# An attention and low-rank mixer kernel whose steps are written out as one list in place of loops

## The chip, the cores and the metric

The kernel runs on one core of one Trainium2 chip. The time is the device time of one execution in microseconds (us). A core has five instruction streams that run side by side and meet at semaphores: TensorE (PE in the profile, with its weight loads shown apart as PEld), VectorE (DVE), ScalarE (ACT), GpSimd (POOL) and SyncE (SP). Transfers are issued from SP, ACT or POOL and carried by 16 shared DMA engines. Each stream works through its own instructions in order; an instruction that waits holds up whatever stands behind it.

## The reference

There are 8 batches, 8 heads, 576 tokens, 64 elements per head, and 16 extra "beacon" keys and values ahead of the tokens. Attention is causal over the tokens; the beacons are seen by all. Then a low-rank mix over tokens (rank 32) and a two-layer network over the 512 channels, with 2048 hidden ones.

```python
k_all = concatenate([beacon_k, k], axis=2)
v_all = concatenate([beacon_v, v], axis=2)
scores = where(causal, -1e9, q @ k_all.T / sqrt(64))
a = exp(scores - scores.max(-1)); a /= a.sum(-1) + 1e-9
x = (a @ v_all) arranged as [batch, token, 8 * 64]
u = x + (x.T @ U @ V).T
out = u + maximum(u @ w_ch1, 0) @ w_ch2
```

## The kernel before, in words

Work on the attention goes by pairs of heads: 4 pairs per batch, 32 pairs, numbered 0 to 31. For a pair,

- k and q are loaded, rounded to 16 bits and regrouped (`regroup`, L230) into a tile of three rotating ones, so that a transpose gives both heads at once;
- PE transposes them into PSUM (L238, L240), and DVE copies the result into `kT` and `qT` (L241, L242). From batch 3 on the transposes are done by DMA from SP instead (`turn_heads` L253, `turn_pair` L260), and DVE reorders the result (L268);
- scores are made in two visits of PE (L294): the first for groups 0 and 1, the second for 2 and 3. ACT takes their exponentials into `expt` (L300), and DVE cuts off the masked part (L281, L283);
- for each head PE multiplies with v (L318), v having a column of ones for the sum, and DVE takes the reciprocal and normalises into `xb` (L326, L327).

When the four pairs of a batch are done, `mix_units` makes the low-rank part: a head (L358, with a cast of its small result, L364), then two parts (L377, L384) whose results ACT and DVE copy into `uT` (L391 to L395). `uT` is a ring of token columns. Each 512 of them make a block of the two-layer network, nine blocks in all: 16 units of the first product (`g_unit`, 4 matmuls each, L418, ReLU shared by ACT and DVE), then 16 units of the second (`c_unit`, L434, each output tile of 128 tokens in four units). These units wait in `queue`, and `fill(n)` emits up to n of them between attention steps, so that PE has work while ACT and DVE treat the scores. An empty queue makes `fill` do nothing.

All PSUM tiles come from one ring of eight. The exponentials of a pair use two of four buffers.

The order is that of the emitted program, engine by engine. Before the change it comes from loops: the first two pairs are written out, then a loop over the pairs of batches 0 and 1 (in which pair p+2 is transposed and scored while pair p is multiplied, with the fill counts in `FIRST`), then a loop over the other pairs with nine fill places each. `mix` puts the three mixing steps of a batch into the queue with the gaps of `GAPS`.

Loads of batch 0: k and q come raw in 32 bits by SP and one ACT issue, in four sets of two heads (`load_first`), and are cast by `group_first` on ACT, DVE or POOL. v of batch 0, and everything of the later batches, comes by POOL's queue, which converts to 16 bits. The order there is: v of batch 0 first half, (POOL casts), v second half, k and q of batch 1 in halves, the beacon keys, v of batch 1 first half, the first weight in two pieces, (casts of U and V on POOL), v of batch 1 second half, the second weight in two pieces, batch 2. U and V themselves come by eight small loads from SP (`small_loads`). `keep_warm` emits matmuls whose result is not used: ten ahead of the first transposes and two or three ahead of the first visits (23 in all).

Of the kernel before, what the change touches and what calls it, by code (L numbers as in the profile page):

```python
# [27 lines left out]
def kernel(  # L28
# [103 lines left out]
    def small_loads():  # L132

        f = utp.tile([P, (NT + 1) * R + S], F32, name="small", tag="ut")
        uf, vf = f[:, 0 : (NT + 1) * R].rearrange("p (j r) -> p j r", r=R), f[:, (NT + 1) * R :]
        nc.vector.memset(uf[0:Nb, 0, :], 0.0)
        nc.sync.dma_start(out=uf[Nb:P, 0, :], in_=moe_U[0 : nq[0], :])
        nc.sync.dma_start(out=uf[: nq[0], NT, :], in_=moe_U[0 : nq[0], :])
        nc.sync.dma_start(
            out=uf[:, 1 : NT - 1, :], in_=moe_U[q0[1] : QM, :].rearrange("(j p) r -> p j r", p=P)  # L140
        )
        nc.sync.dma_start(out=uf[:NL, NT - 1, :], in_=moe_U[QM:S, :])
        for cc in range(NCC):
            nc.sync.dma_start(out=vf[ds(R * cc, R), :], in_=moe_V)
# [87 lines left out]
    def qkT_units(L, pr, qT, kT, c):  # L232
# [3 lines left out]
        def one(i, dst, w):  # L236
# [4 lines left out]
            nc.vector.tensor_copy(out=dst[:, c, 0 : w - 4 * P], in_=ps[:, 0 : w - 4 * P])  # L241
            nc.vector.tensor_copy(  # L242
# [22 lines left out]
    def order_units(raw, qT, kT, c):  # L265

        def one(i, dst, w):
            nc.vector.tensor_copy(  # L268
# [130 lines left out]
    def mlp_units(t0, n, dst, flip, turned=True, last=False):  # L399
# [28 lines left out]
        def c_unit(i, part):  # L428
            m = min(P, n - P * i)
            if part == 0:  # L430
                cps["t"] = pst([P, DM], F32, name="cps")
            ps = cps["t"]
            for dc in range(4 * part, 4 * part + 4):
                nc.tensor.matmul(  # L434
                    ps[:m, :], gT["t"][:, dc, ds(P * i, m)], w2[:, dc, :], start=(dc == 0),
                    stop=turned and dc == NDC - 1, skip_group_check=True,
                )
            if part == 3:
                ob = outp.tile([P, DM], F32, name="ob", tag="ob")
                if not turned:  # L440
                    for cc in range(NCC):
                        nc.tensor.matmul(
                            ps[:m, ts(cc, P)], uT[:, cc, ds(ring(t0) + P * i, m)], ident, start=False, stop=True,
                            skip_group_check=True,
                        )
                if turned:
                    nc.vector.tensor_tensor(out=ob[:m, :], in0=ps[:m, :], in1=gT["u"][:m, i, :], op=ALU.add)  # L447
# [4 lines left out]
                nc.sync.dma_start(out=dst(i, m), in_=ob[:m, :])  # L452

        def half_unit(i, h, part):
            cs = ds(DM // 2 * h, DM // 2)
            if part == 0:
                cps["t"] = pst([P, DM // 2], F32, name="cps")
            ps = cps["t"]
            for dc in range(8 * part, 8 * part + 8):
                nc.tensor.matmul(  # L460
                    ps, gT["t"][:, dc, ds(P * i, P)], w2[:, dc, cs], start=(dc == 0), stop=(dc == NDC - 1)
                )
            if part == 1:
                ob = outp.tile([P, DM // 2], F32, name="ob", tag="ob")
                nc.vector.tensor_tensor(out=ob, in0=ps, in1=gT["u"][:, i, cs], op=ALU.add)
                nc.sync.dma_start(out=dst(i, P)[:, cs], in_=ob)

        units += [lambda dc=dc: g_unit(dc) for dc in range(NDC)]
        for i in range((n + P - 1) // P):
            if last and i == 3:  # L470
                units += [lambda h=h, part=part: half_unit(3, h, part) for h in range(2) for part in range(2)]
                continue
            units += [lambda i=i, part=part: c_unit(i, part) for part in range(4)]
# [30 lines left out]
    def load_batch(b):  # L504
        Ls[b] = qk_tiles()
        emit_loads(b, Ls[b], vss[b % 2])

    HALVES = [slice(0, H // 2), slice(H // 2, H)]
    SETS = [slice(2 * c, 2 * c + 2) for c in range(NH2)]
    raw = {}  # L510
# [26 lines left out]
    def act_copy(out, in_):  # L537
        nc.scalar.activation(out=out, in_=in_, func=AF.Copy)

    prs = {}  # L540

    def group_first(c, i, copy):

        if c not in prs:
            prs[c] = pair_tile()
        regroup(Ls[0], c, i, copy, prs[c])
        hs = SETS[c]
        copy(out=Ls[0][0][i][:NL, hs, :], in_=raw["head"][:NL, i, hs, :])

    def regroup_of(p):  # L550
        b, c = divmod(p, NH2)
        prs[p] = pair_tile()
        for i in range(2):
            regroup(Ls[b], c, i, nc.vector.tensor_copy, prs[p])

# [5 lines left out]
    def new_qT(b):  # L561
        qTs[b] = qkt.tile([P, NH2, S], F16, name="qT", tag="qT")

    def new_qT_of(p):
        b, c = divmod(p, NH2)
        if b not in qTs:
            new_qT(b)

    raw_of = {}

    def turn_of(p):
        b, c = divmod(p, NH2)
        new_qT_of(p)
        if c == 0:
            turn_heads(Ls[b], qTs[b], kTs[b % 2])
        regroup_of(p)
        raw_of[p] = turn_pair(prs[p])

    def qkT_of(p):
        b, c = divmod(p, NH2)  # L580
        new_qT_of(p)
        if p in raw_of:
            return order_units(raw_of[p], qTs[b], kTs[b % 2], c)
        return qkT_units(Ls[b], prs[p], qTs[b], kTs[b % 2], c)

    def scores_of(p):
        b, c = divmod(p, NH2)
        return score_units(c, qTs[b], kTs[b % 2], [expts[(2 * p + i) % NE] for i in range(2)])

    def av_of(p):  # L590
        b, c = divmod(p, NH2)
        if c == 0:
# [3 lines left out]
        return [  # L596
            lambda i=i: av_unit(b, 2 * c + i, expts[(2 * p + i) % NE], vss[b % 2], xbs[b]) for i in range(2)
        ]


    NF = 2
    HB = 3
    HX = 3
    AHEAD = 8
    GAPS = [(0, 3, 3), (0, 3, 3), (5, 7, 2)]
    HINT = 5

    FIRST = [0, 0, 0, 0, 10, 5, 4, 4]

    QUOTA = {2: 4}  # L610

    IDLE = [10, 3, 2, 2]
# [3 lines left out]
    def fill(n):  # L616
        while n > 0 and queue:
            u = queue.pop(0)
            if u is not None:
                u()  # L620
            n -= 1

    def feed(b):

        while state["t"] < NBLK and 512 * (state["t"] + 1) <= S * (b + 1):
            t = state["t"]
            queue.extend(
                mlp_units(512 * t, 512, lambda i, m, t=t: rows[ds(512 * t + P * i, m), :], t % 2, t > 0, t == NBLK - 1)
# [3 lines left out]
    def mix(b):  # L632

        head, parts = mix_units(xbs[b], S * b, xts.get(b))
        seq, rest = [], queue[:]
        for u, n in zip([head] + parts, GAPS[min(b, NF)]):
            seq += rest[:n] + [u]
            rest = rest[n:]
        queue[:] = seq + rest
        feed(b)  # L640

    with tc.manual_schedule(engines={ENG.PE, ENG.Activation, ENG.DVE, ENG.SP, ENG.Pool}):
        load_first()
        v_loads(v[0], beacon_v[0], vss[0], HALVES[0])
        cast_small = small_loads()
# [5 lines left out]
        V, G = nc.vector.tensor_copy, nc.gpsimd.tensor_copy  # L651
        group_first(0, 0, act_copy)
        group_first(0, 1, V)
        keep_warm(pst([P, 512], F32, name="idle"), IDLE[0])
        t0, sc = qkT_of(0), scores_of(0)
        for u in t0:
            u()
        sc[0](IDLE[1])
        sc[1]()
        masks = sc[2]  # L660
        group_first(1, 0, G)
        group_first(1, 1, V)
        v_loads(v[0], beacon_v[0], vss[0], HALVES[1])
        for u in qkT_of(1):
            u()
        sc = scores_of(1)
        sc[0](IDLE[2])
        group_first(2, 0, G)

        Ls[1] = qk_tiles()  # L670
        group_first(3, 0, G)
        k_loads(1, Ls[1], HALVES[0])
        q_loads(1, Ls[1], HALVES[0])
        beacon_load(nc.gpsimd, beacon_k[1], Ls[1][0][0], ALLH)
        k_loads(1, Ls[1], HALVES[1])
        q_loads(1, Ls[1], HALVES[1])
        v_loads(v[1], beacon_v[1], vss[1], HALVES[0])
        emit_w1(0)
        emit_w1(1)
        cast_small()  # L680
        v_loads(v[1], beacon_v[1], vss[1], HALVES[1])
        emit_w2()

        NP1 = NF * NH2
        for p in range(NP1):
            b, c = divmod(p, NH2)
            if c == 0 and NF <= b + 1:
                load_batch(b + 1)
            seq = [masks]
            if p + 1 < NP1:  # L690
                seq.insert(0, sc[1])
                masks = sc[2]
            av, qk, sc = av_of(p), [], []
            if p + 2 < NP1:
                if p == 0:
                    seq.append(lambda: group_first(2, 1, V))
                elif p > 1:
                    seq.append(lambda p=p: regroup_of(p + 2))
                qk = [lambda i=i, p=p: qkT_of(p + 2)[i]() for i in range(2)]
            seq += av[0:1] + qk + av[1:2]  # L700
# [162 lines left out]
```

## Time and profile before

| | us |
|---|---|
| median of 3 runs | 365.34 (365.23 to 365.62) |
| the profiled execution | 368.63 |
| its span, first to last instruction | 367.0 |
| PE busy in the span | 348.5 (95%) |
| DVE busy | 215.0 (59%) |
| ACT busy | 166.3 (45%) |
| POOL busy | 84.0 (23%) |
| mean granted clock of PE | 0.986 |

The profile is of one execution; the span leaves out what lies around it (1.6 us here). A matmul's busy time includes the time in which it runs through the pipeline: 576 matmuls of the first product show 382 ns each, while four of them in a row take 0.86 us from start to start. So a busy PE is no PE at its peak, and the steps below are read from starts in the timeline. "Granted clock" is the share of full speed at which PE's clock runs in a stretch.

### The profile page before, as it was taken

Reading aid. Unit: us, or ns where it says so; the run is one execution under the profiler, and the core shown is the slowest. Engines: PE = TensorE matmul, PEld = TensorE weight load, DVE = VectorE, ACT = ScalarE, POOL = GpSimd, SP = SyncE. Lnnn points to the kernel's source line nnn. Section 1 sums busy time; section 2 is a strip of 40 time slices with the busy share of each in tenths; the row PEclk is TensorE's granted clock in tenths of the full one; section 3 lists DMA queues with packets and bytes.
Section 4 is the critical chain, followed back from the end, with each engine's and each line's share of the span. In section 5 each row is a group of like instructions: output and inputs, shape, how many; then the busy total and the mean of one; then the engine's idle time right before and its main releaser. Section 6 shows DMA issues by size and latency. Waiting matters only on the chain.

```text
span 367.0 us, 7587 instructions
## 1 busy us (share of the span) xinstructions
PE 348.5 (95%) x2956; PEld 171.1 (47%) x2956; DVE 215.0 (59%) x589; ACT 166.3 (45%) x362; POOL 84.0 (23%) x123
## 2 busy tenths in 40 slices
PE   6768999999799999999998999999999999999995
PEld 2546545454345544444443444444444543444443
DVE  4976656467676766585668666676566445223311
ACT  3958660468544475347432653475336201401300
POOL 8977436400371006300440013000000000000000
PEclk9978999999899999999999999999999999999999
DMA  8999999998999946995599529852333023013112
GB/s 176 210 147 174 196 202 145 206 126 113 138 85 204 203 83 62 186 190 113 64 185 202 111 43 126 165 105 49 104 90 65 18 78 100 14 58 86 30 50 74
DMA packets 130987, 43.81 MB, mean 119 GB/s; under 512 B 106624, under 2 KB 125312, under 8 KB 130944
## 3 DMA queue, kind: packets, MB, share of 16 engines
q0 software_dynamic: 65904, 17.54, 53.7%
q1 hardware_dynamic: 64592, 25.41, 33.8%
q8 instruction: 25, 0.41, 0.5%
q10 hardware_dynamic: 448, 0.30, 0.3%
q14 instruction: 18, 0.15, 0.1%
HBM read 37.87 MB, written 9.44 MB: 129 GB/s over the span
## 4 chain that ended last, share of the span: by engine, by line
PE 84%; DMA 6%; DVE 5%; SPq 2%; ACT 1%; POOL 1%; issue 1%; ACTq 0%; POOLq 0%
PE cps L434 33%; PE gps L418 33%; PE po L318 7%; PE sps L294 7%; DMA raw<-pr 2%; DMA hd<-in_q_dram 2%; DMA stm<-in_k_dram 2%; PE cps L460 1%; PE ups L384 1%; ACT expt L300 1%; SPq L167 1%; PE tps L240 1%; PE qtp L358 1%; PE ups L377 1%; DVE gT L424 1%
## 5 line engine op out<-in xcount | busy, mean ns | idle before, releaser
L300 ACT ACTIVATE expt<-sps 128x496 f16<-128x496 f32 (+2 forms) x256 | 111.1, 530 | 77.1 <-PE sps L294 77.1
L418 PE MATMUL gps<-uT,w 128*128 128x512 f16 x576 | 137.7, 382 | 1.2 <-DVE uT L391 1.1
L434 PE MATMUL cps<-w,gT 128*128 128x512 f16 x560 | 130.6, 379 | 0.0
L422 ACT ACTIVATE gT<-gps 128x512 f16<-128x512 f32 x86 | 51.9, 611 | 84.4 <-PE gps L418 82.7
L418 PEld LDWEIGHTS <-w 128*128 128x128 f16 x576 | 52.1, 98 | 62.3 <-issue 7.8
L434 PEld LDWEIGHTS <-gT 128*128 128x128 f16 x560 | 50.9, 98 | 61.3 <-issue 6.0
L424 DVE TENSOR_SCALAR gT<-gps 128x512 f16<-128x512 f32 x58 | 40.0, 689 | 36.3 <-PE gps L418 34.9
L447 DVE TENSOR_TENSOR ob<-cps,ut 128x512 f32<-128x512 f32 x31 | 21.4, 691 | 42.0 <-PE cps L434 41.6
L318 PEld LDWEIGHTS <-expt 128*128 128x128 f16 (+1 forms) x960 | 37.7, 99 | 15.8 <-DVE expt L281 2.2
L180 POOL DMA_DIRECT2D vs<-in_v_dram x50 | 40.6, 826 | 14.6 <-PE po L318 4.4
L318 PE MATMUL po<-vs,expt 128*128 128x65 f16 (+1 forms) x960 | 40.6, 195 | 1.0 <-DVE expt L281 0.5
L294 PE MATMUL sps<-qT,kT 64*128 64x80 f16 (+4 forms) x384 | 34.6, 288 | 5.5 <-DVE kT L242 3.2
L281 DVE TENSOR_TENSOR expt<-expt,bigmask 128x512 f16<-128x512 f16 x64 | 27.1, 423 | 16.4 <-ACT expt L300 15.7
L327 DVE TENSOR_TENSOR xb<-po,rec 128x320 f16<-128x320 f32 x64 | 31.4, 491 | 2.2
L294 PEld LDWEIGHTS <-kT 64*128 64x128 f16 x384 | 12.6, 96 | 32.4 <-issue 16.5
L170 POOL DMA_DIRECT2D vs<-in_beacon_v_dram x10 | 5.4, 535 | 97.1 <-PE po L318 96.8
L326 DVE RECIPROCAL rec<-po 128x5 f32<-128x5 f32 x64 | 12.0, 187 | 19.3 <-PE po L318 18.9
L230 DVE COPY pr<-st 128x512 f16<-128x512 f16 x56 | 15.4, 318 | 1.8 <-DMA st<-in_q_dram 1.5
L391 DVE TENSOR_TENSOR uT<-ups,xt 128x240 f16<-128x240 f32 (+3 forms) x40 | 15.3, 447 | 1.1 <-PE ups L384 1.1
L268 DVE COPY qT<-raw 128x512 f16<-128x512 f16 x20 | 12.3, 617 | 3.7 <-DMA raw<-pr 3.7
L283 DVE TENSOR_TENSOR expt<-expt,mask 80x80 f16<-80x80 f16 x64 | 12.6, 198 | 0.0
L268 DVE COPY kT<-raw 128x512 f16<-128x512 f16 x20 | 12.4, 619 | 0.0
(71 smaller groups left out, 151.4 us busy)
## 6 DMA issues: line engine op xcount, KB each, us to landing
out_dram<-ob SPq DMA_DIRECT2D x35, 256.0 KB, 2.9
w<-in_moe_w_ch_dram POOLq DMA_DIRECT2D x4, 1024.0 KB, 12.1
st<-in_k_dram POOLq DMA_DIRECT2D x6, 512.0 KB, 8.2
st<-in_q_dram POOLq DMA_DIRECT2D x6, 512.0 KB, 11.8
vs<-in_v_dram POOLq DMA_DIRECT2D x18, 128.0 KB, 7.1
stm<-in_k_dram SPq DMA_DIRECT2D x4, 256.0 KB, 4.6
vs<-in_v_dram POOLq DMA_DIRECT2D x12, 64.0 KB, 6.4
stm<-in_q_dram SPq DMA_DIRECT2D x3, 256.0 KB, 6.2
```

The lines of the kernel that those rows point to most:

```text
L180: nc.gpsimd.dma_start(out=dst[a : a + nq[j], j, :, :], in_=src[hs, ds(q0[j], nq[j]), :].rearrange("h p d -> p h d"))
L268: nc.vector.tensor_copy(out=dst[:, c, w - 4 * P : w].rearrange("x (p j) -> x p j", j=4), in_=raw[:, i, :, :].rearrange("x j p -> x p j"),)
L281: nc.vector.tensor_tensor(out=e4, in0=e4, in1=bigmask, op=ALU.min)
L294: nc.tensor.matmul(ps[g, i][:, ds(o, w)], kT[hp, c, ds(P * ch, P)], qT[hp, c, ds(qa, w)], start=True, stop=True,)
L300: nc.scalar.activation(out=ex[i][:, ds(PAD + SLOT * g, gw[g])], in_=ps[g, i][:, 0 : gw[g]], func=AF.Exp, scale=scale)
L318: nc.tensor.matmul(po[:, j, :], ex[0 : nk[c], ds(blk[(c, j)], P)], vs[0 : nk[c], ds(c * H * E + h * E, E)], start=(c == 0), stop=(c == j),)
L327: nc.vector.tensor_tensor(out=xb[:, h // 2, :, ds(D * (h % 2), D)], in0=po[:, :, 0:D], in1=r.broadcast_to([P, NT, D]), op=ALU.mult)
L418: nc.tensor.matmul(g[:, 0:n], w1[:, cc, ts(dc, P)], uT[:, cc, ds(ring(t0), n)], start=(cc == 0), stop=(cc == NCC - 1))
L422: nc.scalar.activation(out=gT["t"][:, dc, 0:n], in_=g[:, 0:n], func=AF.Relu)
L424: nc.vector.tensor_scalar_max(out=gT["t"][:, dc, 0:n], in0=g[:, 0:n], scalar1=0.0)
L434: nc.tensor.matmul(ps[:m, :], gT["t"][:, dc, ds(P * i, m)], w2[:, dc, :], start=(dc == 0), stop=turned and dc == NDC - 1, skip_group_check ...
L447: nc.vector.tensor_tensor(out=ob[:m, :], in0=ps[:m, :], in1=gT["u"][:m, i, :], op=ALU.add)
```

## The change

The loops are replaced by one text, `SCRIPT`, whose words are steps; `step` carries out one word. A number n is `fill(n)`. `Gq` and `Gk` regroup (and in batch 0 cast) q or k of a pair; the letter after them names the engine (V for DVE, A for ACT, G for POOL). `Tq` and `Tk` transpose or reorder, with the engine of the copy in the same place. `Sa` and `Sb` are the two visits of the scores (`:n` adds n unused matmuls), `M` the masks, `A p.i` the product with v of head i, `X b.i` a mixing step, `R` the transposes by DMA, `x` the transpose of a finished `xb`. `k`, `q`, `b`, `v` are loads (with A or B for a half of the heads), `u` the eight small loads, `c` the cast of U and V, `w1i` a quarter of the first weight, `w2i` a half of the second. `I10` is the ten warm-up matmuls.

What differs from before:

- batch 0's pairs and its mixing stand ahead of all transposes and scores of batch 1;
- the casts of batch 0 are shared in another way: q0, k0, k1 by POOL, ahead of v's loads on POOL's queue;
- the small loads come later: a new memset on DVE that touches the whole tile stands ahead of them, and their cast goes from POOL to DVE;
- the first weight comes in quarters (the second, then the first quarter, ahead of the second half of batch 1), the second in halves by output columns; the first block's second product works in half-width pieces, all tokens for the first half of the columns, then for the second;
- some regroupings and copies after transposes go to ACT, in batches 0 to 5;
- the mixing steps stand in the list itself and not in the queue. Unit by unit, the first batches are in another order; from pair 19's first visit on, the order of matmuls is the old one;
- the unused matmuls are 19 instead of 23.

```diff
     def small_loads():
...
+        nc.vector.memset(f.rearrange("p (a b) -> p a b", b=R)[:, :, 0:1], 0.0)
         nc.vector.memset(uf[0:Nb, 0, :], 0.0)
...
-        def cast():
+        def cast(copy):
             for rr, jj in ((P, slice(0, NT - 1)), (NL, slice(NT - 1, NT)), (nq[0], slice(NT, NT + 1))):
-                nc.gpsimd.tensor_copy(out=Usb[:rr, jj, :], in_=uf[:rr, jj, :])
-            nc.gpsimd.tensor_copy(out=Vsb, in_=vf)
+                copy(out=Usb[:rr, jj, :], in_=uf[:rr, jj, :])
+            copy(out=Vsb, in_=vf)
...
     def emit_w1(i):
         w1r = moe_w_ch1.rearrange("(cc p) f -> p cc f", p=P)
-        fs = ds(FF // 2 * i, FF // 2)
+        fs = ds(FF // 4 * i, FF // 4)
         nc.gpsimd.dma_start(out=w1[:, :, fs], in_=w1r[:, :, fs])

-    def emit_w2():
+    def emit_w2(i):
         w2r = moe_w_ch2.rearrange("(dc p) c -> p dc c", p=P)
-        for i in range(2):
-            dcs = ds(NDC // 2 * i, NDC // 2)
-            nc.gpsimd.dma_start(out=w2[:, dcs, :], in_=w2r[:, dcs, :])
+        cs = ds(DM // 2 * i, DM // 2)
+        nc.gpsimd.dma_start(out=w2[:, :, cs], in_=w2r[:, :, cs])
...
-            nc.vector.tensor_copy(out=dst[:, c, 0 : w - 4 * P], in_=ps[:, 0 : w - 4 * P])
-            nc.vector.tensor_copy(
+            copies[i](out=dst[:, c, 0 : w - 4 * P], in_=ps[:, 0 : w - 4 * P])
+            copies[i](
                 out=dst[:, c, w - 4 * P : w].rearrange("x (p j) -> x p j", j=4),
                 in_=ps[:, NL:SK].rearrange("x (j p) -> x p j", j=4),
             )
...
-        def c_unit(i, part):
+        def c_unit(i, cs, w, part, parts):
...
+        todo = [(i, 0, DM) for i in range(nt)]
+        if halves:
+            todo = [(i, h, DM // 2) for h in (0, DM // 2) for i in range(nt)]
...
+    COPY = {"V": nc.vector.tensor_copy, "G": nc.gpsimd.tensor_copy, "A": act_copy}
...
+    def mix_of(b, part):
+        if b not in mixes:
+            head, parts = mix_units(xbs[b], S * b, xts.get(b))
+            mixes[b] = [head] + parts
+        mixes[b][part]()
+        if part == 2:
+            feed(b)
...
+    SCRIPT = """
+        GqG0 GkG0 I10 GkG1 TqV0 v0A TkA1 v0B GqV1 TkV0 GkV3 Sa0:3 GkV2 TqV1 Sb0 2 TkA3 Sb1 M0 GqV2 1 u q1A
+        Sa1:2 GqV3 A0.1 TqV2 TkV2 k1A A0.0 M1 Sa2:2 w11 cV w10 b1 Sb2 q1B TqV3 A1.0 1 A1.1 Sa3:2 1 w12 Sb3 v1A
+        GqA4 M2 GkA5 A2.0 A2.1 v1B w13 w20 M3 k1B A3.0 GqA5 A3.1 w21 GkV4 X0.0 X0.1 X0.2 TqV4 TkA4 1 q2 1 GqA6
+        1 k2 TqV5 3 Sa4 1 TkA5 Sb4 2 M4 b2 Sb5 1 TqA6 2 A4.1 2 Sa5 1 A4.0 2 GkV7 GqA7 M5 1 GkA6 TkV6 TkV7 TqA7
+        A5.0 1 A5.1 Sa6 Sb6 4 M6 1 GqV8 2 A6.1 Sb7 GkA9 1 v2 Sa7 1 GkA10 b3 q3 k3 A6.0 M7 2 A7.0 GkA8 TkV9
+        GqV10 1 A7.1 1 X1.0 X1.1 1 GqV9 X1.2 TqV8 TqA9 TkV8 1 Sa9 v3 2 Sb8 5 TqA10 1 Sa8 1 M8 Sb9 2 TkA10 M9 1
+        A8.1 A8.0 GqV13 Sa10 GkV11 GkA13 1 GkV12 k4 Sb10 GqV12 GqA11 R12 1 A9.0 2 TkA11 TqA11 3 A9.1 GkV14 b4
+        Sb11 M10 1 Sa11 TqV12 A10.0 M11 2 A10.1 TkV12 q4 GqV14 2 R13 Sb12 1 Sa12 GkA15 GqV15 M12 1 R14 1 A11.0
+        A11.1 v4 TkA13 TqV13 R15 A12.0 1 TqV14 b5 1 Sa13 1 k5 TkV14 1 GqV16 GkA16 Sb13 q5 1 A12.1 X2.0 Sb14 1
+        M13 2 Sa14 A13.0 1 TkV15 GqV18 A13.1 2 x13 TqA15 X2.1 X2.2 GqV17 GkV17 Sb15 R16 1 R17 1 M14 2 x12
...
+    """
...
+        for t in SCRIPT.split():
+            step(t)
```

More of the change, by code (lines that the diff above doesn't have):

```diff
@@ L627, in feed @@
             queue.extend(
[L628 removed]
+                mlp_units(512 * t, 512, lambda i, m, t=t: rows[ds(512 * t + P * i, m), :], t % 2, t > 0, t == NBLK - 1, t == 0)
             )
             state["t"] += 1
[L632 to L640, printed above, removed]
+    def mix_of(b, part):
[5 more added lines that the diff above has]
+            feed(b)
```

302 lines of the change are left out of this document (114 added, 188 removed).

## The prediction

> **What bounds the kernel now.** I read the page's slices first, then the busy time by stretches of the span, then the timeline of the first 40 us, the waits, and the engine queues of PE, POOL and SP. In the page's slices (40 of 9.2 us; a digit is the busy share, or the granted clock, in tenths):
>
> ```profile
> PE   6768999999799999999998999999999999999995
> PEclk9978999999899999999999999999999999999999
> ```
>
> PE is full from the fifth slice on; the room is in the first four, in the slice at 92 to 101 us and in the last. The busy time by stretches (columns: length, then busy us and instructions of PE, PEld, DVE, ACT, POOL; granted clock, DMA share, GB/s):
>
> ```profile
> 21.20:23.40 2.20, 0.00 (x0) 0.00 (x0) 0.63 (x3) 2.09 (x6) 1.24 (x3) 0.83 1.56 189
> 23.40:27.00 3.60, 3.56 (x33) 2.23 (x35) 3.37 (x12) 0.16 (x1) 3.60 (x6) 0.50 1.24 98
> ...
> 35.90:97.00 61.10, 58.19 (x573) 29.91 (x572) 37.90 (x111) 32.89 (x74) 22.95 (x29) 1.00 1.50 162
> 97.00:101.00 4.00, 4.00 (x29) 1.59 (x29) 3.71 (x12) 2.43 (x5) 0.00 (x0) 0.60 1.33 153
> ```
>
> A gap of 2.2 us is followed by half clock, and 97 to 101 shows it again: a PE that looks busy and does half. Lines of the timeline fix the head (start, length, engine, line):
>
> ```profile
> 7.36 0.44 SPq L173 DMA_DIRECT2D stm<-in_k_dram  x1
> 13.65 0.62 POOL L230 CAST pr<-stm 128x512 f16<-128x512 f32 x1 [0.20 <-DMA stm<-in_k_dram]
> 13.52 2.26 SPq L144 DMA_DIRECT2D small<-in_moe_V_dram  x4
> 23.43 0.25 PE L238 MATMUL tps<-ident,hd 80*128 80x80 f16 x1 [2.28 <-DMA hd<-in_q_dram]
> 35.88 1.89 PE L418 MATMUL gps<-uT,w 128*128 128x512 f16 x8
> 160.79 0.58 PE L294 MATMUL sps<-qT,kT 64*128 64x496 f16 x4
> ```
>
> The fourth set of k, issued at 7.36, lands at 13.5. PE stands until 23.4 for batch 1's q, which the loop order wants before batch 0 is done. The first MLP matmul is at 35.88. At 160.79 comes the first half of pair 19's scores. Writing both orders out unit by unit, I find the same units before that point and the same order after it. So **the change is decided before 160.8 us**; the tail (the last output, 355 to 367) is common.
>
> **The ledger.** Change = shift of the first MLP matmul + attention work deferred past it + wider bookkeeping - old stalls gone + new stalls. The work between 35.9 and 160.8 (124.9 us) is otherwise taken over as it is.
>
> **First MLP matmul in the new list.** DVE runs its list in order, so I follow that queue. Prices from the timeline's rows: a transposed half of a pair copied out 0.79 (0.19 and 0.68, overlapped), a cast of a raw set 0.65 (0.43 and 0.22), a pair's masks 0.97, a head's reciprocal and product 0.70.
> - The ten warm-up matmuls end at 5.9 as before; q of pair 0 is transposed and copied by 7.1. The cast of q set 1 waits for its landing (8.63 before; I take 8.3, since v no longer loads beside it) and ends 9.1, k of pair 0 at 9.9.
> - Next on DVE stands the cast of k set 3. Landing: at the earliest 7.36 + 3.2 (the shortest stm landing) = 10.6, at the latest 13.5 as now; I take 12.5, nearer the row. Behind it wait the cast of k set 2 and q of pair 1: 12.5 + 0.65 x 2 + 0.79 = 14.6. Masks of pair 0 to 15.6, q set 2 to 16.2. Only now comes the new memset, and it holds back all eight small loads of U and V, which SP issued from 10.46 on before.
> - v's first half moves behind three POOL casts: six issues of 4.2 us from 7.4, so the last starts at 10.8 and lands 6.4 later (median of its row), at 17.2. Pair 0's first product with v follows: 12.54 before, 17.2 now. It takes 0.6; then on DVE 0.70, two copies 1.58, 0.70 and masks 0.97: 21.8.
> - Next is the cast of U and V, moved from POOL to DVE. SP needs about 3.3 us to reach its last small issue (0.31 to 0.57 each): 16.3 + 3.3 = 19.6, and it lands 5.7 later (its row's median; 5.2 to 6.2), at 25.3. **DVE stands 3.5 us**, and behind the wait are pair 3's q copy (hence pair 3's scores), pair 1's normalising and every later mask. The cast itself has no DVE row: between two POOL casts of it (1.26) and the 128x512 DVE cast alone (0.42); I take 0.95.
> - From 26.25: q copy 0.79, two heads 1.40, masks 0.97, two heads 1.40, masks 0.97 = 31.8; the last product, its normalising and the first batch's mixing take 4.6 more (product 0.5, normalising two heads 1.0 after it, low-rank head and its cast 0.9, two parts of PE 1.3, copies 0.9): **36.4**, against 35.9.
>
> Bounds: 32.9 if the small loads cost no wait (36.4 - 3.5); 38.9 with k set 3 at 13.5, landings of 6.2 and PE at half clock in the last links. The first weight pieces do not bind: issued by POOL at 19.5 and 20.4, they land by 33.0 even at the longest weight landing (12.6, for pieces twice as large). If they bound, each us late is a us. On POOL the rest of batch 1 and the other pieces follow: by the same issue times (1.4 for a half of k or q, 4.2 for one of v, 0.9 for weights) the third piece goes at 23.2, the fourth at 32.5, the first half of the second weight at 33.4, k's second half at 34.3. Landings of up to 12.6 put them at 36, 45, 46 and 47; they are wanted from 43, 47, 55 and 56 on at the earliest, so they are hidden with 2 us to spare, less if POOL has to wait as it did for 1.9 and 4.9 us ahead of the second weight.
>
> **Deferred.** Before, PE had by 35.9 also transposed pair 5, scored pairs 4 and 5 and made one product of pair 4: 2 x 0.225 + 2 x 1.03 (scores 0.92 and 0.11 for the slower change back to a full-height matmul) + 0.46 = **3.0**. The first block's second product in half-width pieces: 128 at 0.109 (row L460: 3.66 less one latency over 31) less 64 at 0.2155 = **0.2**. Its extra small outputs lie beside PE work.
>
> **Old stalls gone.** Pair 12's transposes by DMA are issued about 11 us ahead of their use (seven MLP units of 0.86 and 4 us of attention lie between; the landing was 7.6, after 2.5 for the head rows). That frees the idle 1.9 at 94 to 96.5 and about 1.6 lost to half clock until 101: **3.5**; 4.4 at most with the small mask waits near 53 and 57.
>
> **New stalls.** (a) PE does some 14 us of work between 6 and 36, so it starts the MLP at half clock: 1.7 by the stretch after 97, up to 3.1 by the 6.3 us after 23. I take **1.7**. (b) After block 0 the filler queue is empty where batch 1 is mixed: normalising, low-rank head, copies in a row, 4 us against 3.3 us of PE work: **0.7** (0 to 2). (c) Before batch 2 is mixed, the queue is empty for about eight fill places. From pair 13's second scores ACT has exps 1.55 + 1.55 + 1.95, a copy 0.7, and the two parts' copies 0.8 + 0.9, behind a latency 0.4: 7.8 us, while PE has 5.0 of work: **2.8** (1.5 to 5). In the stretch between both mixings ACT comes to about 41 us of work (seven pairs of exps at 3.45, ten ReLUs at 0.61, its new copies) beside 44 of PE, so it has little room; no more is charged for that.
>
> **Sum**: 0.5 + 3.0 + 0.2 - 3.5 + 5.2 = +5.4 us. The profiled execution took 368.63 (span 367.0 and 1.6 around it), so 374.0 of its kind; the runs' median is 365.34, 3.3 below, and the difference carries over: **370.7 us**.
>
> **Rivals.**
> - *The head runs without its waits* (faster). The deciding place is the U and V cast: if the small loads land by 21.8, it costs nothing, and with k set 3 at 11 and v 1.4 earlier the MLP starts at 31.5. With 0.5, 0.5 and 1.5 for the new stalls and 4.4 gained: -4.4 + 3.2 - 4.4 + 2.5 = -3.1, **362.2**. Break-even with the stalls as I sized them is a first MLP matmul at 31.0. For it: SP's queue is empty by then, and the early DMA load is lighter. Against: 5.2 to 6.2 us for every small landing, and the weights now run beside them.
> - *Half clock through the head* (slower still). The last product, low-rank head and mixing sit on the path and take nearly double (a head's products 1.03 against 0.62 at 24.4), +1.7, and the slow stretch after the start is the longer one, +1.4: **373.8**. For it: half clock from 23 to 29 after 2.2 us without a matmul. Against: the many short bursts may keep the clock up, as from 6 to 21. [...]
> - *ACT piles up* (slowest). Its new copies stand in order before exps; if masks and products wait for it through the middle, the 3 us of room become a like deficit and (c) goes to 5: about +6 more, **377**. It decides from ACT over 95% busy between 70 and 115 us.
> - *The two sides cancel*: the start near 31 to 32, stalls as sized: **365.3**, no change. That the list does not do what it says is this case too: batch 0 first, yet the MLP no sooner.
>
> **Chances.** Forecast 0.48 (own range 367 to 373), half clock 0.15, ACT 0.10, cancelling 0.06, faster 0.21. The range leaves out half of the faster case's lower side and the worst of ACT: **362 to 378**. A difference under 0.2% (0.7 us) cannot be told from none here; so faster 0.21, same 0.06, slower 0.73.
>
> **What would show it.** The first MLP matmul's start (36.4; under 31 and I am wrong); DVE idle ahead of the U and V cast and the cast of k set 3, with DMA as releaser; pair 0's first product near 17; no raw transpose wait near pair 12; PE idle before block 2's first matmul; pair 19's scores at about 166 instead of 160.8. If these scores come before 160, the ledger's head is wrong; if the head is right and they do not come at 166, the new stalls are.

## The result, and the profile after

| | before | changed |
|---|---|---|
| median (us) | 365.48 (365.23 to 366.14) | 375.59 (375.07 to 376.50) |
| ratio, 95% interval | | 1.028 (1.025 to 1.030) |
| the profiled execution | 368.63 | 376.50 |
| its span | 367.0 | 374.8 |
| first MLP matmul | 35.88 | 39.14 |
| first visit of pair 19's scores | 160.79 | 165.83 |
| from there to the end of the span | 206.2 | 209.0 |
| mean granted clock | 0.986 | 0.967 |

The changed kernel is slower by 10.1 us in the runs and by 7.8 us between the two spans. 3.3 us of the 7.8 are there at the first MLP matmul, 5.0 at pair 19; 2.8 come behind it. Medians and ratios below leave out four slow runs: one of e1, two of e8 and one of the kernel before beside e8. The page's slices after the change (40 of 9.4 us, as before):

```profile
PE   6648999999989999999997999999999999999995
PEclk9685899999999999999999899999999999999999
```

The later slice with PE at 7 tenths has moved from 92 to 197 us, the second and third are emptier than before, and the clock is at 6, 8, 5 and 8 tenths in the second to fifth. The timeline of the changed kernel (start, length, engine, line, operation, count; in brackets the idle time before it and what ended it):

```profile
12.18 0.43 DVE L230 CAST pr<-stm 128x512 f16<-128x512 f32 x1 [3.19 <-DMA stm<-in_k_dram]
15.43 0.08 DVE L136 MEMSET small<- 128x24 f32 x1
16.74 1.01 PE L318 MATMUL po<-vs,expt 128*128 128x65 f16 x15
26.20 0.46 DVE L150 CAST Vsb<-small 128x576 f16<-128x576 f32 x1 [4.21 <-DMA small<-in_moe_V_dram]
27.40 1.57 PE L294 MATMUL sps<-qT,kT 64*128 64x496 f16 x12 [4.42 <-DVE qT L242]
32.05 1.83 PE L318 MATMUL po<-vs,expt 128*128 128x65 f16 x30 [1.14 <-DVE expt L281]
38.72 0.63 PE L240 MATMUL tps<-ident,pr 128*128 128x128 f16 x4
39.14 2.99 PE L418 MATMUL gps<-uT,w 128*128 128x512 f16 x12
...
107.90 0.29 DVE L230 COPY pr<-st 128x512 f16<-128x512 f16 x1 [1.82 <-DMA raw<-pr]
108.58 0.63 PE L318 MATMUL po<-vs,expt 128*128 128x65 f16 x15 [1.50 <-DVE expt L281]
...
165.83 0.58 PE L294 MATMUL sps<-qT,kT 64*128 64x496 f16 x4
...
205.36 1.61 PE L418 MATMUL gps<-uT,w 128*128 128x512 f16 x4 [1.95 <-DVE uT L391]
```

Read from the top: DVE stands for k set 3, then for U and V; behind that cast is the copy of pair 3's q, and with it PE stands 4.42 us. The last product of batch 0 starts at 32.05, and from there the mixing takes 7.1 us. Later there are two stalls of PE: one at 108 that was not there before, and one of 1.95 us at 205. The line of the kernel before for the second:

```profile
199.13 1.61 PE L418 MATMUL gps<-uT,w 128*128 128x512 f16 x4 [1.11 <-DVE uT L391]
```

Busy time by stretches shows what the clock does (length, busy of PE, PEld, DVE, ACT, POOL; granted clock, DMA share, GB/s):

```profile
30.00:40.00 10.00, 8.28 (x108) 6.31 (x106) 6.46 (x20) 4.98 (x13) 8.12 (x12) 0.52 1.35 118
200.00:210.00 10.00, 7.49 (x58) 2.86 (x57) 7.19 (x20) 3.74 (x9) 0.00 (x0) 0.84 1.41 198
```

PE looks 83% busy from 30 to 40 and runs at about half speed (granted clock 0.52).

### The profile page after: what moved, and what is told of

It reads as the page before. It is cut to its first block, busy times and chain, and to the rows that moved or that the text cites. A ratio compares the mean times of both kernels' runs of the same rounds, so it can differ in the third digit from the quotient of the medians.

```text
span 374.8 us, 7696 instructions
## 1 busy us (share of the span) xinstructions
PE 352.1 (94%) x3016; PEld 180.7 (48%) x3016; DVE 199.3 (53%) x553; ACT 188.2 (50%) x407; POOL 83.6 (22%) x121
## 4 chain that ended last, share of the span: by engine, by line
PE 85%; DMA 6%; DVE 3%; SPq 2%; ACT 1%; issue 1%; DVEq 0%
PE gps L418 34%; PE cps L435 33%; PE po L318 7%; PE sps L294 6%; DMA raw<-pr 2%; DMA small<-in_moe_V_dram 2%; DMA sth<-in_k_dram 1%; ACT expt L300 1%; DMA stm<-in_q_dram 1%; PE tps L240 1%; PE ups L384 1%; PE ups L377 1%; PE qtp L358 1%; DVE expt L281 1%; DVE uT L391 1%
## 5 line engine op out<-in xcount | busy, mean ns | idle before, releaser
L418 PE MATMUL gps<-uT,w 128*128 128x512 f16 x576 | 135.2, 381 | 2.1 <-DVE uT L391 2.0
L435 PE MATMUL cps<-w,gT 128*128 128x512 f16 (+1 forms) x656 | 134.4, 353 | 0.0
L435 PEld LDWEIGHTS <-gT 128*128 128x128 f16 x656 | 60.3, 98 | 56.6 <-issue 4.1
L418 PEld LDWEIGHTS <-w 128*128 128x128 f16 x576 | 52.9, 98 | 67.3 <-issue 9.1
L448 DVE TENSOR_TENSOR ob<-cps,ut 128x512 f32<-128x512 f32 (+1 forms) x33 | 22.3, 674 | 50.1 <-PE cps L435 50.0
L318 PEld LDWEIGHTS <-expt 128*128 128x128 f16 (+1 forms) x960 | 38.6, 101 | 15.9 <-DVE expt L281 3.6
L294 PE MATMUL sps<-qT,kT 64*128 64x80 f16 (+4 forms) x384 | 36.2, 293 | 6.5 <-DVE qT L242 4.9
L173 POOL DMA_DIRECT2D st<-in_k_dram x8 | 7.0, 875 | 39.2 <-DVE rec L326 23.1
L230 DVE COPY pr<-st 128x512 f16<-128x512 f16 x39 | 11.1, 315 | 1.8 <-DMA raw<-pr 1.8
L268 DVE COPY qT<-raw 128x512 f16<-128x512 f16 x16 | 9.7, 606 | 3.9 <-DMA raw<-pr 3.9
```

The lines of the kernel that those rows point to most:

```text
L294: nc.tensor.matmul(ps[g, i][:, ds(o, w)], kT[hp, c, ds(P * ch, P)], qT[hp, c, ds(qa, w)], start=True, stop=True,)
L318: nc.tensor.matmul(po[:, j, :], ex[0 : nk[c], ds(blk[(c, j)], P)], vs[0 : nk[c], ds(c * H * E + h * E, E)], start=(c == 0), stop=(c == j),)
L418: nc.tensor.matmul(g[:, 0:n], w1[:, cc, ts(dc, P)], uT[:, cc, ds(ring(t0), n)], start=(cc == 0), stop=(cc == NCC - 1))
L435: nc.tensor.matmul(ps[:m, :], gT["t"][:, dc, ds(P * i, m)], w2[:, dc, ds(cs, w)], start=(dc == 0), stop=turned and dc == NDC - 1, skip_gro ...
```

## The experiments

All but before_again are the changed kernel with other words in its list. Theory A, from the prediction: the new order sets instructions that wait for late loads ahead of others in DVE's queue, and this is what the head loses. The other letters: B, the pieces and the bookkeeping cost (quarters of the weight, half-width first block); E, the fill queue is empty around batch 4's mixing, behind pair 19; G, the copies given to ACT cost. "Rest" is the time from the first MLP matmul to the end of the profiled span; it is 331.1 us before the change and 335.7 after. Kernels between two lines share the runs of the kernel before, whose median stands with the first.

| run | median | ratio to before, 95% | span | first MLP matmul | rest |
|---|---|---|---|---|---|
| e1_old_order_as_list (before: 367.43) | 364.28 | 0.992 (0.988 to 0.996) | 363.7 | 34.86 | 328.8 |
| e2_small_first | 370.54 | 1.011 (1.006 to 1.017) | 369.5 | 33.88 | 335.6 |
| e3_keep_clock | 374.85 | 1.022 (1.015 to 1.028) | 373.6 | 38.24 | 335.4 |
| e4_two_fills | 374.38 | 1.025 (1.018 to 1.032) | 372.3 | 36.47 | 335.8 |
| --- | | | | | |
| before_again (before: 365.10) | 365.84 | 1.002 (0.999 to 1.005) | 366.8 | 36.37 | 330.4 |
| e5_old_head | 373.30 | 1.023 (1.019 to 1.028) | 371.6 | 35.60 | 336.0 |
| e6_copies_on_dve | 382.43 | 1.045 (1.041 to 1.050) | 382.1 | 38.08 | 344.0 |
| e7_small_first_k3_later | 370.76 | 1.016 (1.012 to 1.021) | 369.2 | 33.95 | 335.3 |
| --- | | | | | |
| e8_old_head_no_wait (before: 366.30) | 369.04 | 1.007 (1.003 to 1.012) | 366.5 | 28.48 | 338.0 |
| e9_old_head_fills | 365.70 | 0.998 (0.995 to 1.002) | 362.9 | 28.17 | 334.7 |
| e10_v_first | 369.60 | 1.010 (1.006 to 1.013) | 367.9 | 32.43 | 335.5 |
| --- | | | | | |
| e11_best (before: 365.12) | 362.80 | 0.991 (0.988 to 0.995) | 362.0 | 28.47 | 333.5 |

**The old order, written as a list** (e1). All else of the change stays: weights in quarters, half-width first block, the step words.

```diff
     SCRIPT = """
-        GqG0 GkG0 I10 GkG1 TqV0 v0A TkA1 v0B GqV1 TkV0 GkV3 Sa0:3 GkV2 TqV1 Sb0 2 TkA3 Sb1 M0 GqV2 1 u q1A
+        v0A u GkA0 GqV0 I10 TqV0 TkV0 Sa0:3 Sb0 GkG1 GqV1 v0B TqV1 TkV1 Sa1:2 GkG2 GkG3 k1A q1A b1 k1B
...
```

> The steps of the kernel before, unit by unit in its old order and on its old engines, written as a list; the first weight still comes in quarters, the second in halves by columns, and block 0's second product works in half-width pieces. If it is the new order that costs (theory A): 365.5 us and no more than 0.5 off. If the pieces or the half-width product cost (rival B): most of the 10 us loss stays, 370 or more.

It comes out no slower than before, even a little faster: pieces, half-width block and list cost nothing, and B falls. What costs is the order, that of the loads included, together with the engines it names. In this execution of e1 the first MLP matmul waits for its weight and not for batch 1's q:

```profile
34.86 1.90 PE L418 MATMUL gps<-uT,w 128*128 128x512 f16 x8 [0.78 <-DMA w<-in_moe_w_ch_dram]
```

**The small loads first** (e2). The memset and the eight loads of U and V go to the front; their cast stays where the change put it.

```diff
-        GqG0 GkG0 I10 ... 1 u q1A
+        u GqG0 GkG0 I10 ... 1 q1A
```

> The changed kernel with the small loads of U and V (and the memset ahead of them) put first in the list, so that SP issues them from about 10 us on as before. Theory A: the wait of 4.2 us ahead of the cast of V goes, pair 3's scores start about 4 us sooner, the first MLP matmul comes at about 35 instead of 39.1 and the kernel is 3 to 4 us faster than the changed one: 372. Rival C (the head is bound by something beside it: masks, exps, v's landing): first MLP matmul at 38 or later, 375.

```profile
21.25 0.45 DVE L150 CAST Vsb<-small 128x576 f16<-128x576 f32 x1
33.88 1.46 PE L418 MATMUL gps<-uT,w 128*128 128x512 f16 x6
```

No wait stands at the cast any more, and the first MLP matmul comes 5.3 us earlier, as does the end of the span (374.8 to 369.5). This one word is worth half of the loss or more (the ratio falls from 1.028 to 1.011), and more than the 3 to 4 us expected. Pair 3's scores come 4.4 us sooner (22.96 against 27.40), and the 30 matmuls of pair 2's products behind them run at full clock here (1.09 us) and at half clock in the changed kernel (1.81). From the last product on, e2 runs at half clock as well:

```profile
26.90:33.80 6.90, 6.30 (x87) 4.99 (x88) 3.81 (x13) 3.00 (x8) 3.40 (x5) 0.51 1.52 189
```

**Keeping the clock** (e3). Unused matmuls fill PE's gaps in the head (41 of them); the waits stay.

```diff
-        Sb0 2 TkA3 ... A1.0 1 A1.1 Sa3:2 1 w12 Sb3 v1A ... A2.0 A2.1 v1B
+        Sb0 I12 2 TkA3 ... A1.0 1 A1.1 I18 Sa3:2 1 w12 Sb3 I6 v1A ... A2.0 A2.1 I5 v1B
```

> The changed kernel with 41 more unused matmuls in four places where PE stands in the head (12 after pair 0's second scores, 18 after pair 1's products with v, 6 after pair 3's scores, 5 after pair 2's products). If half clock stretched the head's last links (theory D): granted clock near 1.0 from 12 us on, the first MLP matmul 2 to 3 us earlier than 39.1 and block 0 starting at full clock, 372 us. If the links wait for DVE and ACT anyway: 39.1 stays and only the first MLP matmuls gain, 374.5.

```profile
28.40 2.74 PE L218 MATMUL idle<-ident 128*128 128x512 f16 x6
33.51 1.09 PE L318 MATMUL po<-vs,expt 128*128 128x65 f16 x30 [0.23 <-DVE expt L281]
38.24 2.10 PE L418 MATMUL gps<-uT,w 128*128 128x512 f16 x9
```

Only 0.9 us is gained at the first MLP matmul, where 2 to 3 were expected. The rows say why. From the last product to the MLP it now takes 4.7 us instead of 7.1, so half clock is worth 2.4 us there. But the six fillers behind pair 3's scores still ran at half clock, took 2.74 us (the next five, at 32.03, took 1.24) and pushed the products behind them: the last one starts at 33.51 instead of 32.05. A filler ahead of needed work is itself work.

**Two fills less before pair 19** (e4), so that the queue still has two units at batch 4's mixing.

```diff
-        2 GkA21 A18.0 1 R21 q6 1
+        1 GkA21 A18.0 R21 q6 1
```

> The changed kernel with two fill places taken out near pair 18, so that from pair 19 on the MLP units lie as in the kernel before, and the filler queue does not run empty ahead of batch 4's second mixing part. Theory E: the 2.8 us that the changed kernel loses after pair 19's first scores (span +7.8 against +5.0 there) come from the two empty fill places at 201 to 210 us; without them the span is 372.0 and the time 372.8. Rival: they come from elsewhere, and the time stays at 375.6.

```profile
173.77 0.62 PE L318 MATMUL po<-vs,expt 128*128 128x65 f16 x15 [2.87 <-DVE gT L424]
204.44 1.61 PE L418 MATMUL gps<-uT,w 128*128 128x512 f16 x4 [1.11 <-DVE uT L391]
```

At 204 the wait falls to the 1.11 us it was before the change. The same units are now missing at pair 18, where a wait of 2.87 appears. The place of E is right; the edit robbed another. (Its first MLP matmul is 2.7 us early since the small loads landed earlier in that execution: DVE waited 1.7 us for them. So its span of 372.3, where 372.0 was expected, is no sign for E.)

**The kernel before, again.**

> The kernel before, unchanged, profiled once more. Its first profiled execution took 368.6 us where its runs took 365.3. If the two gaps of that profile (2.2 us ahead of 23.4, and the one at 94 to 96.5, each with half clock behind it) belong to that execution alone (theory F), one of them at least is shorter here, the span is near 364 and the first MLP matmul still near 35.5. If they belong to the kernel, both are there and the span is 366 to 368.

```profile
36.37 3.46 PE L418 MATMUL gps<-uT,w 128*128 128x512 f16 x8 [2.28 <-DMA w<-in_moe_w_ch_dram]
```

In this execution the head waits 2.28 us for the weights. Where the first profile had 2.28 us for q, PE waits 1.44 us, at 22.3, and the profile names ACT's exponentials; the first MLP matmul is within half a microsecond of the first profile's. The second gap is there too, but shorter than the 1.89 us of the first profile, and with full clock behind it (1.00 from 97 to 101, where it was 0.60):

```profile
98.09 0.58 PE L294 MATMUL sps<-qT,kT 64*128 64x496 f16 x4 [1.45 <-DVE gT L424]
```

Both gaps are shorter, as F has it, yet the span is 366.8 and not near 364, since the wait for the weights is new. Of 70 runs of the kernel before, the 21 with a mean clock of 0.998 or more have a median of 364.99, the 11 with 0.993 or less one of 368.10. The profiled execution of the prediction, 368.63 at 0.986, was of the second kind, and so is this one, 368.60 at 0.991. No execution of the first kind was profiled.

**The old head** (e5): up to batch 0's mixing the old order and engines, except that batch 1's transposes and scores stay behind it and weight quarters come ahead of batch 1.

```diff
+        v0A u GkA0 GqV0 I10 TqV0 TkV0 Sa0:3 Sb0 ... Sb3 M2 A2.0 A2.1 w13 w20 GkV4 GqV4 M3 k1B v1B A3.0
+        GkV5 GqV5 A3.1 w21 X0.0 X0.1 X0.2 TqV4 TkA4 1
```

> Batch 0 as in the kernel before (same engines, v first, small loads at once, pairs in turn), but without pairs 4 and 5 in between, the first two quarters of the first weight right behind v; U and V cast on POOL; from pair 4 on the changed kernel's list with pair 4 and 5 regrouped on DVE. Theory A (batch 0's new order in the head costs, the rest of the list hardly): pair 3's exps end near 23.5, the first MLP matmul at 28 to 30, and from there to the end 335.6 us as in the four profiles of the new list so far: span 364 to 366, 10 us under the changed kernel. If the weights bind instead, the first MLP matmul stands waiting for them at 31 or later. Rival (the order from pair 4 on costs): first MLP matmul early, but more than 338 us from there to the end.

```profile
27.14 0.66 DVE L230 COPY pr<-st 128x512 f16<-128x512 f16 x2 [4.10 <-DMA st<-in_k_dram]
28.20 1.83 PE L318 MATMUL po<-vs,expt 128*128 128x65 f16 x30 [6.08 <-DVE expt L281]
```

A miss, and the same trap built anew: `GkV4 GqV4` stand ahead of `M3`, batch 1's k is late, DVE waits 4.10 us with pair 3's masks behind it, and PE 6.08. The first MLP matmul is at 35.6 instead of 28 to 30.

**All copies back on DVE** from pair 4 on (e6): `GqA6` becomes `GqV6`, and so on.

> The changed kernel with all regroupings and copies that it gave to ACT from pair 4 on put back on DVE. Theory G (ACT is too full between 85 and 130): the gap of 1.5 us at 107 to 108.6 and those near 126 and 128.7 shrink, and 1 to 2 us are gained: 374. If sharing pays: DVE gets later with the copies out of PSUM, and 1 to 3 us are lost: 377.

```profile
172.65 0.98 PE L294 MATMUL sps<-qT,kT 64*128 64x496 f16 x4 [2.54 <-DVE kT L268]
```

7 us slower than the changed kernel, more than either side expected: PE waits for DVE's copies. Sharing them with ACT pays in this order, and G falls.

**Small loads first, k set 3 later** (e7): as e2, with the casts of k sets 2 and 3 behind pair 0's masks.

```diff
-        TkV0 GkV3 Sa0:3 GkV2 TqV1 Sb0 2 TkA3 Sb1 M0 GqV2 ... Sa1:2 GqV3 A0.1
+        TkV0 Sa0:3 TqV1 Sb0 Sb1 M0 GkV2 GqV2 ... Sa1:2 GkV3 GqV3 TkA3 A0.1
```

> The changed kernel with the small loads first and, besides, the casts of k sets 2 and 3 moved on DVE behind pair 0's masks, the transposes of pair 3's k accordingly. If k set 3's landing at 12.2 is the next thing that holds the head: pair 0's masks done by 13 instead of 15, first MLP matmul 1.5 to 2 us earlier than with the small loads alone (33.9): 32, and 368.5. If v's landing or ACT holds it: first MLP matmul at 33 to 34, 370.

```profile
16.14 0.32 PE L318 MATMUL po<-vs,expt 128*128 128x65 f16 x5 [0.43 <-DMA vs<-in_v_dram]
17.06 0.22 PE L318 MATMUL po<-vs,expt 80*128 80x65 f16 x1 [0.60 <-DMA vs<-in_v_dram]
```

The wait for k set 3 is gone and nothing is gained (33.95 against 33.88), the second of the two expectations: pair 0's product then waits for v, which the change moved behind POOL's casts, and is done at 17.3.

**The old head without the wait** (e8) and **the same with two fills moved** (e9). In e8 batch 1's first regroupings stand behind the mixing, and six fillers cover pair 3's exponentials. e9 gives the two units back from two places, one each.

```diff
 e8
-        A2.0 A2.1 w13 w20 GkV4 GqV4 M3 k1B v1B A3.0 GkV5 GqV5 A3.1 w21 X0.0 X0.1 X0.2 TqV4 TkA4 1 q2 1
+        A2.0 A2.1 I6 w13 w20 M3 k1B v1B A3.0 A3.1 w21 X0.0 X0.1 X0.2 GkV4 GqA4 2 GkA5 GqV5 TqV4 TkA4 q2 1
 e9, besides
-        A18.1 2 x18 ... A19.1 2 x19
+        A18.1 1 x18 ... A19.1 1 x19
```

> The old head once more (order and engines of batch 0, v and the small loads ahead of the casts), then the new order, but batch 1's first regroupings stand behind batch 0's mixing instead of ahead of pair 3's masks, where VectorE waited 4.10 us for batch 1's k in the run before; six filler matmuls keep TensorE at work while pair 3's exponentials run. Theory A, in-order waits of VectorE for late loads are what the new head loses: the first MLP matmul at 28.5 to 30.5 us, and with the 335.3 to 336.0 us that every kernel with the new list takes from there to the end, a span of 364 to 366.5 and a median of 365 to 368. Rival W, the weights can't come earlier: the first MLP matmul waits for them until about 35 (release by a weight DMA), span near 371. Rival L, the list from pair 4 on only waits elsewhere when it starts earlier (batch 1's k and q land at a fixed time): the first MLP matmul is early, but from there to the end it takes 339 or more.

> As the kernel beside it, with one fill unit each taken from behind pair 18 and behind pair 19, so that the queue still has two units around batch 4's mixing. Theory E, the empty places there cost 1.6 to 2.5 us: TensorE's wait for uT near 200 falls to about 1.1 us with the full clock after it, no new wait over 1 us near pairs 18 and 19, span 1.5 to 2.5 us shorter than the kernel beside it. Rival, every unit of the queue covers some wait, and what is gained there is lost where the unit is missing: spans within 0.7 us of each other, a new wait of 1 us or more between 165 and 195.

The timeline of e8, then of e9:

```profile
28.48 1.89 PE L418 MATMUL gps<-uT,w 128*128 128x512 f16 x8 [0.53 <-ACT uT L395]
196.64 1.89 PE L418 MATMUL gps<-uT,w 128*128 128x512 f16 x4 [1.94 <-DVE uT L391]
```

```profile
195.03 1.61 PE L418 MATMUL gps<-uT,w 128*128 128x512 f16 x4 [1.11 <-DVE uT L391]
```

And the busy time by stretches, of e8 and of e9 (the granted clock is the third number from the end):

```profile
196.00:204.00 8.00, 7.36 (x37) 2.98 (x38) 4.56 (x12) 2.64 (x6) 0.00 (x0) 0.62 1.40 175
```

```profile
196.00:204.00 8.00, 7.96 (x57) 3.49 (x56) 4.94 (x12) 4.98 (x12) 0.00 (x0) 1.00 1.30 200
```

With no late load in front of DVE's work the MLP starts at 28.5, 10.7 us earlier than in the changed kernel, at full clock, as A has it; but e8 also gives batch 0 its old order and engines back, so it does not show the waits' share alone (e10 does). The weights are there in time, so W falls. But the end of the span is only 8.3 us earlier, and the median stays above the 365 to 368 expected: the rest took 338.0, between A's 336.0 and L's 339. Its largest item is E, for e9 takes 3.6 us off the span and 3.3 off the median, more than the 2.5 expected: besides the wait it takes away about 6 us of half clock behind it (0.62 over 8 us, then 1.00). No wait of 0.6 us or more appears between 160 and 190.

**v first as well** (e10): e7, with v's first half ahead of pair 0's casts, and those on DVE and ACT.

```diff
-        u GqG0 GkG0 I10 GkG1 TqV0 v0A TkA1
+        v0A u GkA0 GqV0 I10 GkG1 TqV0 TkA1
```

> The new order with three loads put back: the small loads ahead of all, the first half of v ahead of pair 0's casts on POOL's queue (these go to VectorE and ScalarE as before), k set 3's cast behind pair 0's masks. The list is otherwise the new one. Theory A: with all three waits out of VectorE's queue pair 0's product starts near 13 to 14 instead of 17, the first MLP matmul comes at 30 to 32 instead of 34, span 365.5 to 367.5. Rival K, the last links to the first MLP matmul hang on the half clock or on ScalarE's 62 exponentials and not on v: 33 to 34, span 369 as with the small loads first alone.

```profile
16.55 0.63 PE L318 MATMUL po<-vs,expt 128*128 128x65 f16 x15
32.43 1.89 PE L418 MATMUL gps<-uT,w 128*128 128x512 f16 x8
```

Between the two expectations: 1.5 us earlier than e7 at the MLP, 1.3 in the span. The product no longer waits for v, yet starts at 16.55 and not at 13 to 14: pair 1's scores and the transposes of k set 3, with the cast that they need, stand ahead of it in the list. Of the 4 us that still lie between e10 and e8, 2.9 are there at the last product (26.30 against 23.41) and 1.1 come behind it (6.1 us to the MLP against 5.1), where e10's clock is 0.53 from 28.8 to 32.4 and e8's 1.00. So of e8's 10.7 us the late small loads are 5.3 (e2), v's place with its casts 1.5, k set 3 nothing that shows, and the last 4 the rest of batch 0's order and the clock, which no run parts further.

**One more wait** (e11). Looking for what is left in e9, the rows near pair 10 (DVE, then PE) show where the stall at 108 of the changed kernel comes from:

```profile
98.89 0.29 DVE L230 COPY pr<-st 128x512 f16<-128x512 f16 x1 [2.21 <-DMA raw<-pr]
99.09 0.42 DVE L281 TENSOR_TENSOR expt<-expt,bigmask 128x512 f16<-128x512 f16 x1
...
99.57 0.62 PE L318 MATMUL po<-vs,expt 128*128 128x65 f16 x15 [1.90 <-ACT expt L300]
```

The regrouping of pair 14 waits for the transposing DMA of pair 12, the only one issued by then (at 90.21; it landed 8.6 us later), and pair 10's masks wait behind it. That it takes over that DMA's source buffer is read from this wait. The profile names ACT's exponentials for PE's wait, but PE needs the masks too. e11 moves that regrouping behind pair 11's masks, and the cast of U and V from POOL to ACT.

```diff
-        w12 cG v1A Sb3 M2 ... A9.1 GkV14 b4 Sb11 M10 1 Sa11 TqV12 A10.0 M11 2
+        w12 v1A Sb3 cA M2 ... A9.1 b4 Sb11 M10 1 Sa11 TqV12 A10.0 M11 GkV14 2
```

> The kernel with the old head and the two fills moved, with two more edits. First, the regrouping of k for pair 14 moves from ahead of pair 10's masks to behind pair 11's masks: in every kernel with the new list VectorE waits there 1.78 to 2.09 us for the transposing DMA of pair 12 (raw<-pr), whose buffer the regrouping takes over, and TensorE stands 1.5 to 1.9 us behind the masks. Second, the cast of U and V goes from POOL, where it stood until 25.1 behind a weight load, to ScalarE behind pair 3's exponentials. Theory A, these are in-order waits in front of work that others need: TensorE's wait near 99.5 (1.90 us) is gone and no new one over 1 us appears before 130; the wait for Usb (1.05) falls under 0.5; span 360 to 361.5 against 362.9, median 1.5 to 2.5 us below that kernel's, ratio to the kernel before 0.990 to 0.996. Rival, ScalarE's backlog and not VectorE's wait holds pair 10's product (the profile puts TensorE's wait down to ScalarE's exponentials): the wait stays above 1.2 us there, span 362.4 or more.

```profile
97.78 0.58 PE L294 MATMUL sps<-qT,kT 64*128 64x496 f16 x4
98.29 0.63 PE L318 MATMUL po<-vs,expt 128*128 128x65 f16 x15
...
99.51 0.61 DVE L268 COPY qT<-raw 128x512 f16<-128x512 f16 x1 [1.27 <-DMA raw<-pr]
```

The stall is gone: PE goes from pair 11's scores straight to pair 10's product, and DVE waits for the DMA only behind the masks, where its data is used. So it was DVE's wait and not ACT's backlog. The wait for Usb turned into one of 0.65 us for `xb`, a small miss, and the span fell by 0.9 us, to 362.0, where 360 to 361.5 was expected; half clock in the first 20 us of that execution (0.91 on average there, 1.00 in e9) took part of it. The median, 362.8, is 2.9 below e9's, in another set of runs, and seven of the nine executions have the expected span, 360.6 to 361.5; the profiled one has the lowest clock of them (0.992). e11 beats the changed kernel and, at 0.991 (0.988 to 0.995), the one before. e1, with the old order, stands at 0.992 (0.988 to 0.996): which of the two is better is open.

## Why the prediction was right, and where it was not

The direction was right, and so was the mechanism in the head: DVE's waits for late loads. The size was not: 5.4 us were forecast and 10.1 measured. 375.59 lies 4.9 us above the forecast of 370.7 and outside its own range of 367 to 373; the range of 362 to 378 holds it by the room left for the half-clock and ACT rivals. At the first MLP matmul 0.5 was forecast and 3.3 measured, from there to pair 19 4.9 and 1.8, behind pair 19 nothing and 2.8, between spans and medians nothing and 2.3. By its steps:

1. **DVE's queue in the head: right.** k set 3's cast was put at 12.5 and came at 12.18; pair 0's product at 17.2, came at 16.74 (this one by luck: PE shows no wait for v there, and e10, with v early, starts it at 16.55); the wait of the U and V cast 3.5 us and its end 26.25, were 4.21 and 26.66; the last product 31.8, came at 32.05. That the cast is the deciding place, as the first rival said, e2 shows: 5 us. That k set 3's wait costs anything, e7 does not bear out; v's late landing hides it.
2. **"The last product, its normalising and the first batch's mixing take 4.6 more": mis-sized.** They took 7.1, and the first MLP matmul at 39.14 lies just above the upper bound of 38.9. Half clock is 2.4 of the 7.1 by e3, whose same stretch takes 4.7 (clock 0.93 from 30 to 40). That is the half-clock rival, which I had beside the forecast and not in it: the clock is 0.50 from 27.4 to 39.1, behind PE's gap of 4.42 us. With DVE standing 3.5 us in my own ledger and pair 3's scores behind it, full clock in the stretch that follows was the wrong assumption.
3. **New stalls, 5.2: over-sized up to pair 19.** From the first MLP matmul to pair 19 it took 126.7 us, 1.8 more than before; by my terms (3.0 + 0.2 - 3.5 + 5.2) it would have been 4.9 more. The MLP's start at half clock, an estimate of mine from the stretches behind two gaps, cost about 0.2 instead of 1.7 (the clock is 0.87 until 41 and 1.00 from there to 100), batch 1's mixing 0.3 instead of 0.7 (PE's only wait from 46 to 104, 0.26), and the room before batch 2's mixing was almost enough (0.85 us idle from 120 to 130 instead of 2.8). The 1.5 at 108 was in no term. So the two errors of 2 and 3 cancel, and pair 19 came at 165.8 where I had said 166: a sign that came true for partly wrong reasons.
4. **"Pair 12's transposes by DMA are issued about 11 us ahead of their use": too far, and blind to the buffer.** The issue is at 99.62 and the use at 109.00, and 1.82 us of these are the new wait at 108, for the same DMA, by the regrouping that takes over its source buffer. The old wait for the transposed data is hidden behind it; with the regrouping moved, e11 shows 1.27 us of it on DVE, and 0.19 on PE. I had said no such wait would be seen.
5. **"The same order after it": wrong.** The tail was 2.8 us longer. The order of the matmuls agrees, but at batch 4's mixing two fill places find the queue empty: the list had spent two units earlier. The wait for uT is 1.95 instead of 1.11, a wait of 0.39 at 202 for the copy of an output is new, and the clock is 0.76 from 205 to 212, which is 1.7 us: together about the 2.8. e9 against e8 shows that the two missing units cost 3.6 us. I had the expansion, with those empty places in it, and compared the order of what was there instead of the gaps.
6. **"The difference carries over": wrong by 2.3 us.** The spans differ by 7.8, the medians by 10.1. The profiled execution of the kernel before lay 3.2 us above its median, that of the changed kernel 0.9. The runs of the kernel before show that such executions are mostly those with a lower clock (median 368.10 at 0.993 or less, 364.99 at 0.998 or more). "Old stalls gone", 3.5, was read from one of them: in before_again the same wait is 1.45 with no half clock behind it. So a part of what the change was to take away is not in every execution; how much of it a typical one has is not shown.
7. **ACT piles up: did not happen.** From 70 to 115 us, where over 95% was to decide it, ACT is busy 31.6 of 45, and e6 shows that its copies save 7 us.

Not tried: the changed kernel's head with its clock kept and without fillers in front of needed work, and e1 with e8's head start, which would part the deferred attention work (3.0) from the stalls in the rest.

## What to carry to other kernels

When an instruction is moved up in the list of an in-order engine, ask when its data lands, including the buffer that it overwrites, and what stands behind it; a late transfer at the front of DVE's queue cost PE 4.4 us (U and V), 6.1 (e5) and 1.5 to 1.9 (pair 14) here, each time by way of another pair's masks or copies. Expand both orders with the empty fill places shown, not only the work. And before a stall in a single profile is counted as gain, look whether the median execution has it: compare the profiled time and clock with those of the other runs.

## What the hardware showed unexpectedly

The length of PE's gap alone does not say whether the clock drops. Gaps of 1.94 us (e8, at 197), 1.95 us (changed kernel, at 205) and even 1.31 us (e2, at 26.9) were followed by half clock (0.50 from 196.6 to 202; 0.96 until 207, then 0.50 to 210; 0.51 from 26.9 to 33.8), gaps of 1.90 (e9, at 99.6), 1.50 (changed kernel, at 108.6) and even 2.87 us (e4, at 174) by full clock (1.00 from 99.5 to 106, from 108.5 to 114 and from 173.7 to 183). The stretch behind e4's gap, then the one behind e8's:

```profile
173.70:176.00 2.30, 2.23 (x23) 1.14 (x22) 1.90 (x9) 0.60 (x1) 0.00 (x0) 1.00 0.78 151
```

```profile
196.60:199.00 2.40, 2.36 (x8) 0.56 (x8) 1.66 (x4) 0.00 (x0) 0.00 (x0) 0.50 1.37 183
```

What else decides it is not shown: no run here moved a gap alone.
